# Retention attention and a snake feed-forward layer on one core: later chunks in 64x64 quads, state in SBUF, two sequences loaded whole

## The chip, the cores and the metric

The kernel runs on 1 core of one Trainium2 chip. The metric is device time in microseconds (us), lower is better. A run lists the span of the core and the mean clock granted to TensorE; runs more than 1.5% above the fastest of their kernel are called slow and are left out of comparisons. A profile covers one execution, whose span is about 1.8 us shorter than the time that the run reports.

The engines, as the profile names them: PE is TensorE (matmuls), PEld its weight loads, DVE is VectorE, ACT is ScalarE, POOL is GpSimd, SP is SyncE. In the kernel text, tiles of `psum` lie in PSUM, where the matmuls write; the others (`big`, `work`, `consts`) lie in SBUF, the working memory. The inputs are float32 and are cast to bf16 on the way in, by loads that GpSimd issues.

## The reference

Four sequences of 768 tokens, 8 heads of width 64, go through retention (linear attention with a decay for each head), and the result through a feed-forward layer with a snake activation.

```python
def _attn_ref(q, k, v):                      # each (4, 8, 768, 64)
    gamma = 1.0 - 2.0 ** (-5.0 - np.arange(H))
    for t in range(S):
        state = gamma * state + k[:, :, t] (outer) v[:, :, t]      # 64x64 for each head
        y[:, :, t] = q[:, :, t] @ state / sqrt(D)

def _moe_ref(x, w_in, w_out, alpha):         # x: 3072 tokens x 512, d_ff 2048
    h = x @ w_in
    s = np.sin(alpha * h)
    g = h + s * s / (alpha + 1e-09)
    return g @ w_out
```

(The first function is abridged: the einsums of the original are written as products.)

## The kernel before

The tokens are cut in 24 chunks of 128. The first chunk of each sequence is e0 to e3; `P` is the order of work: first the four first chunks, then chunks 1 to 5 of each sequence. A chunk's attention has four parts on TensorE: scores of the chunk with itself (`stage_A`), the part from the state of the chunks before it, the mix of masked scores with v, and the sums of k times v that go into the state (`stage_S`). All are matmuls of 64 rows or 64 columns, which run in pairs on two half tiles. The decays are divided out of v beforehand (`scale_v`) and multiplied back in when the chunk leaves PSUM (`qg`), so that the state in PSUM is a plain running sum.

```python
def load_chunk(j, names="qkv"):              # three loads of 128 partitions x 8 heads: 1024 runs each
    # ... (tiles)
    nc.gpsimd.dma_start(out=t, in_=chunk_of(src, j))

def turn(j):                                 # the transpose of q and k by DMA
    nc.sync.dma_start_transpose(out=st["qkT", j], in_=raw["qk", j].rearrange("p i h d -> p (i h d)"))

def stage_A(j):                              # scores, then the mask on DVE
    # ...
    for p in range(NP):
        for e in range(2):
            r = slice(64 * e, 64 * e + 64)
            nc.tensor.matmul(pa[:, e, p, :], qkT[r, NP + p, :], qkT[r, p, :], ...)
    nc.vector.tensor_mul(aT, pa, m)          # (rearranges cut)

def keep_S(j, ps):                           # ScalarE copies the sums from PSUM to the weights s_bd
    for e in range(2):
        r = slice(64 * e, 64 * e + 64)
        nc.scalar.copy(s_bd[(j % NCH + 1) % 2][r, :, r], ps[r, :, :])

def stage_M(j):                              # state part, mix, sums, exit to xT
    # ...
    nc.vector.tensor_mul(x, py, qg[:, c])
    if ps is not None:
        keep_S(j, ps)
```

The feed-forward (FF) work is done in groups of tiles of 128 tokens, of sizes 4, 2, 4, 4, 4, 4, 2. In each of a group's slots four FF matmuls make one hidden block (`ph`), ScalarE takes sine and square, DVE adds (`gT`), and TensorE does output matmuls (`po`) of the group before. The attention of the next group's chunks stands between slots:

```python
def phase(g, outs, att, nf=1):
    for n in range(FF // nf):
        now = Slot(g, n * nf, nf=nf).sq("A")
        for fn in att.get(n, ()):            # attention of chunks of the next group
            fn()
        now.add()
        # ... output matmuls of the group before

load_chunk(P[7])                             # GpSimd's order: loads and v decays
load_chunk(P[8])
scale_v(P[6], nc.gpsimd)
# ... loads and decays one after the other to the last chunk

phase(1, outs,                               # the two-tile group; T: transpose on TensorE, X: by DMA
      {0: [T(P[6]), X(P[8])], 1: [A(P[6])], 2: [T(P[7]), X(P[9])], 3: [A(P[7]), M(P[6])], 4: [X(P[10])],
       5: [A(P[8]), M(P[7])], 6: [X(P[11]), A(P[9]), M(P[8]), SK(e1)], 7: [M(P[9])]}, 2)
```

## Time and profile before

| | before |
|---|---|
| median of 3 runs | 219.79 us (218.58 to 219.89) |
| span of the profiled execution | 217.5 us |
| first FF matmul, last matmul (starts) | 15.49, 213.03 us |
| two-tile group starts | 48.21 us |
| the four four-tile groups after it start | 65.09, 90.94, 123.43, 155.67 us |
| last two-tile group starts | 185.54 us |

The starts are those of the first FF matmul of each group, read in the order in time of TensorE. They serve as milestones: the same matmul exists in every kernel, so the difference of two neighbouring milestones is the length of one stage, and a change of the total can be split by stage. The first stages as stretches, with the busy time of each engine:

```profile
core 0: us, PE busy (x) PEld busy (x) DVE busy (x) ACT busy (x) POOL busy (x), PEclk, DMA share, GB/s
48.20:65.10 16.90, 15.64 (x222) 12.03 (x225) 14.06 (x25) 14.40 (x33) 15.42 (x18) 1.00 2.00 161
65.10:90.90 25.80, 24.91 (x213) 12.40 (x216) 18.49 (x25) 22.63 (x41) 20.87 (x23) 1.00 1.93 149
90.90:185.50 94.60, 93.02 (x693) 45.24 (x704) 52.72 (x68) 74.38 (x129) 20.91 (x23) 1.00 0.72 81
```

From 90.9 us on, TensorE is busy nearly all the time (93.02 of 94.60).

### The profile page before, as it was taken

The page shows a single profiled execution, that of the slowest core. Times are in us where ns is not written, and L with a number is a line of the kernel's source. Part 1 is how long each engine was busy: PE and PEld are TensorE (multiplying, and loading weights), DVE is VectorE, ACT ScalarE, POOL GpSimd, SP SyncE. Part 2 cuts the span into 40 slices and gives each one's busy share as a digit, 9 for nine tenths or more (in the row PEclk, how much of TensorE's full clock was granted, in tenths as well). Part 3 has the DMA queues.
Part 4 walks back from the last instruction along what each step waited for, and adds up shares of the span by engine and source line. Part 5 has one row for each costly group of instructions (what it writes and reads, how often), then busy time and mean ns, then how long its engine had stood idle before and what let it go on. Part 6 is the DMA issues. An engine that isn't in the chain of part 4 may idle for free.

```text
span 217.5 us, 4218 instructions
## 1 busy us (share of the span) xinstructions
PE 203.8 (94%) x1634; PEld 107.5 (49%) x1661; DVE 128.1 (59%) x213; ACT 162.8 (75%) x311; POOL 90.1 (41%) x105
## 2 busy tenths in 40 slices
PE   7798899999989999999999999999999999999992
PEld 3444554467764545445455445454544544555540
DVE  4686659867895767766466566366464555233310
ACT  7678796658889999789768768777868876766610
POOL 8975335999889885896981000000000000000000
PEclk9999999999999999999999999999999999999999
DMA  9999999999999999999999146237011101111121
GB/s 132 151 193 191 205 207 164 154 207 161 164 151 182 163 120 154 112 160 175 135 188 107 23 96 77 60 60 96 7 47 51 48 0 51 48 48 48 51 94 50
DMA packets 99508, 24.67 MB, mean 113 GB/s; under 512 B 92304, under 2 KB 96416, under 8 KB 99488
## 3 DMA queue, kind: packets, MB, share of 16 engines
q0 software_dynamic: 77024, 13.37, 84.0%
q1 hardware_dynamic: 22464, 11.02, 26.4%
q8 instruction: 13, 0.21, 0.4%
q14 instruction: 7, 0.06, 0.1%
HBM read 27.27 MB, written 6.29 MB: 154 GB/s over the span
## 4 chain that ended last, share of the span: by engine, by line
PE 74%; DVE 9%; DMA 4%; POOL 4%; ACT 4%; issue 3%; POOLq 0%; ACTq 0%
PE po L304 35%; PE ph L279 31%; DMA qkr<-in_k_dram 4%; DVE gT L294 4%; PE py L247 3%; PE pa L213 2%; POOL qkr L83 2%; ACT s L282 2%; DVE aT L217 2%; PE py L251 2%; POOL vr L83 1%; DVE xT L258 1%; PE ps L227 1%; DVE s L289 1%; ACT s L287 1%
## 5 line engine op out<-in xcount | busy, mean ns | idle before, releaser
L294 DVE SCALAR_TENSOR_TENSOR gT<-s,rec_alpha,ph 128x512 bf16<-128x512 f32 (+3 forms) x120 | 74.1, 637 | 68.1 <-ACT s L287 67.5
L279 PE MATMUL ph<-xT,w_in 128*128 128x512 bf16 (+3 forms) x478 | 97.9, 336 | 1.1 <-DVE gT L294 0.6
L304 PE MATMUL po<-w_out,gT 128*128 128x512 bf16 x360 | 94.1, 379 | 3.8 <-issue 2.9
L282 ACT ACTIVATE s<-ph,alpha_sb 128x512 f32<-128x512 f32 (+3 forms) x120 | 69.6, 601 | 34.0 <-PE ph L279 33.9
L279 PEld LDWEIGHTS <-w_in 128*128 128x128 bf16 x480 | 45.5, 98 | 42.6 <-issue 2.1
L287 ACT ACTIVATE s<-s 128x512 f32<-128x512 f32 (+1 forms) x94 | 58.4, 621 | 2.6
L304 PEld LDWEIGHTS <-gT 128*128 128x128 bf16 x384 | 35.2, 98 | 38.2 <-issue 0.6
L112 POOL TENSOR_TENSOR vr<-vr,kg 128x512 bf16<-128x512 bf16 x21 | 22.0, 1056 | 12.2 <-DMA vr<-in_v_dram 12.2
L217 DVE TENSOR_TENSOR aT<-pa,mask 128x1024 bf16<-128x1024 f32 x20 | 24.4, 1220 | 0.3 <-PE pa L213 0.3
L83 POOL DMA_DIRECT2D vr<-in_v_dram x24 | 21.7, 904 | 3.0 <-DMA w_in<-in_moe_w_in_dram 1.7
L83 POOL DMA_DIRECT2D qkr<-in_q_dram x23 | 21.3, 925 | 4.0 <-DMA w_out<-in_moe_w_out_dram 1.6
L83 POOL DMA_DIRECT2D qkr<-in_k_dram x23 | 20.4, 887 | 3.8 <-DMA w_out<-in_moe_w_out_dram 3.3
L234 ACT CAST s_bd<-ps 64x256 bf16<-64x256 f32 x40 | 14.4, 360 | 2.4 <-PE ps L227 2.1
L316 ACT COPY o_sb<-po 128x512 f32<-128x512 f32 x23 | 13.1, 576 | 3.9 <-PE po L304 3.9
L258 DVE TENSOR_TENSOR xT<-py,qg 128x512 bf16<-128x512 f32 x20 | 13.7, 684 | 2.6 <-PE py L251 2.5
L328 PE MATMUL spare<-warm 128*128 128x512 bf16 x27 | 9.3, 465 | 1.4 <-DVE warm L131 1.2
L213 PEld LDWEIGHTS <-qkT 64*128 64x128 bf16 x192 | 5.4, 94 | 9.3 <-issue 7.1
L251 PE MATMUL py<-aT,vr 128*64 128x128 bf16 x192 | 9.5, 220 | 0.4 <-DVE rec_alpha L366 0.2
L213 PE MATMUL pa<-qkT 64*128 64x128 bf16 x192 | 9.5, 219 | 0.4 <-ACT qkT L186 0.2
L247 PE MATMUL py<-qkT,s_bd 128*64 128x128 bf16 x160 | 8.3, 224 | 0.7 <-DVE xT L258 0.7
L247 PEld LDWEIGHTS <-s_bd 128*64 128x64 bf16 x160 | 5.4, 109 | 4.8 <-issue 2.0
L251 PEld LDWEIGHTS <-vr 128*64 128x64 bf16 x192 | 6.9, 110 | 1.3 <-issue 1.0
(59 smaller groups left out, 68.8 us busy)
## 6 DMA issues: line engine op xcount, KB each, us to landing
out_dram<-o_sb SPq DMA_DIRECT2D x24, 256.0 KB, 2.3
vr<-in_v_dram POOLq DMA_DIRECT2D x24, 128.0 KB, 6.2
qkr<-in_q_dram POOLq DMA_DIRECT2D x23, 128.0 KB, 5.6
qkr<-in_k_dram POOLq DMA_DIRECT2D x23, 128.0 KB, 5.8
w_in<-in_moe_w_in_dram POOLq DMA_DIRECT2D x4, 512.0 KB, 11.1
w_out<-in_moe_w_out_dram POOLq DMA_DIRECT2D x4, 512.0 KB, 14.8
q<-in_q_dram SPq DMA_DIRECT2D x1, 256.0 KB, 3.4
k<-in_k_dram SPq DMA_DIRECT2D x1, 256.0 KB, 4.7
```

What stands on the lines that cost most here:

```text
L83: nc.gpsimd.dma_start(out=t, in_=chunk_of(src, j))
L112: eng.tensor_mul(raw["v", j], raw["v", j], kg[:, j % NCH, :, None].to_broadcast([128, H, D]))
L213: nc.tensor.matmul(pa[:, e, p, :], qkT[r, NP + p, :], qkT[r, p, :], start=(p == 0), stop=True, skip_group_check=True)
L217: nc.vector.tensor_mul(aT.rearrange("p e n t -> p (e n) t"), pa.rearrange("p e n t -> p (e n) t"), m)
L247: nc.tensor.matmul(py[r, p, :], s_bd[c % 2][:, p, r], qkT[:, p, :], start=(p == 0), stop=True, skip_group_check=True)
L251: nc.tensor.matmul(py[64 * e:64 * e + 64, p, :], vs[:, 2 * p + e, :], aT[:, e, p, :], start=(c == 0 and p == 0), stop=True, skip_group_che ...
L258: nc.vector.tensor_mul(x, py, qg[:, c])
L279: nc.tensor.matmul(self.ph[:, m, :], w_in[:, i, f * 128:(f + 1) * 128], xT[g][:, i, self.lo:self.hi], start=(m == 0 and i == 0), stop=(i = ...
L282: nc.scalar.activation(out=self.s[:, m, :], in_=self.ph[:, m, :], func=ACTF.Sin, scale=alpha_sb[:, f:f + 1])
L287: nc.scalar.activation(out=self.s, in_=self.s, func=ACTF.Square)
L294: nc.vector.scalar_tensor_tensor(gT[self.g][:, f, self.lo:self.hi], self.s[:, m, :], rec_alpha[:, f:f + 1], self.ph[:, m, :], op0=ALU.mult ...
L304: nc.tensor.matmul(po[g, ts], gT[g][:, f, ts * C:(ts + 1) * C], w_out[:, f, :], start=(f == 0), stop=(f == FF - 1))
```

## The change

The intent is fewer and shorter matmul bursts for attention. Queries, keys and values of the later chunks are arranged so that four 64x64 tiles of the array work at once (in the "narrow" chunks, those of sequences 0 and 1, this holds for the state part and the scores; their mix and sums stay on two half tiles); for the later chunks of sequences 2 and 3 ("wide" chunks) tokens are split in halves of 64, the empty corner of the scores is left out, and the state part is a full-array matmul. For that the rows of the result are ordered differently (so `w_in` is loaded with some halves of rows swapped), the state sits in SBUF (`s_f`, summed by DVE), and sequences 2 and 3 are loaded whole, head by head. All of one chunk's state part and mix and the next chunk's scores form one burst. Some decays go to DVE; the eighth, eleventh and twelfth chunks are transposed on TensorE (before: the seventh and eighth, the others by DMA; the fifth and sixth on TensorE in both), two early output tiles lie in the scores' PSUM banks, and the last output tile leaves in three pieces.

```diff
+    def load_seq(bt):                       # 24 loads of 64 partitions x 10 blocks: 640 runs each
+        for i, src in enumerate((q, k, v)):
+            for h in range(H):
+                # ...
+                nc.gpsimd.dma_start(out=o, in_=src[bt, h, C:, :].rearrange("(f i) d -> i f d", i=64))
@@
-        nc.gpsimd.dma_start(out=w_in[:, :, ...], in_=w_in_v[:, :, ...])
+        nc.gpsimd.dma_start(out=w_in[:, 0:2, c], in_=w_in_v[:, 0:2, c])
+        for y in range(2):
+            nc.gpsimd.dma_start(out=w_in[64 * y:64 * y + 64, 2:4, c], in_=w_in_v[64 - 64 * y:128 - 64 * y, 2:4, c])
@@ the state
+    def keep(j, py, base=256):
+        # ... first chunk: copy
+            nc.vector.tensor_add(s_f, s_f, new)
+    def hand_on(j):
+        if not wide(j + 1):
+            nc.scalar.copy(s_n[i], s_f)
+            return
+        nc.gpsimd.tensor_copy(s[half(0), :, 0:4:3], s_f[half(0)])
+        nc.gpsimd.tensor_copy(s[half(1), :, 1:3], s_f[half(1)])
@@ attention
+    def inter(j):                           # wide: 4 matmuls of the full array
+    def scores(j, tag="pa"):                # 64x64 tiles, four at a time
+    def mix(j, first=None):                 # wide: the same, narrow: half tiles; and the sums
+    def burst(old, new, first=None):
+        inter(old)
+        return {**scores(new), **mix(old, first)}
@@ GpSimd's order
+    load_chunk(P[11])
+    scale_v(P[9], nc.gpsimd)
+    load_chunk(P[12])
+    load_chunk(P[13])
+    load_seq(2)
+    load_seq(3)                             # the first wide decay and state copy come behind these
@@ the two-tile group
     phase(1, outs,
+          {0: [A(P[6]), X(P[9])], 1: [B(P[6], P[7])], 3: [B(P[7], P[8])],
+           5: [B(P[8], P[9], e1)], 6: [T(P[10])], 7: [B(P[9], P[10])]}, 2, calm=False, hold=6)
@@ the end
-    for fn in out_pieces(NG - 1, range(sizes[-1])):
+    for fn in out_pieces(NG - 1, range(sizes[-1] - 1)):
         fn()
+    last_tile(NG - 1, sizes[-1] - 1)        # 256, 128 and 128 columns
```

## The prediction

> **What bounds the kernel now.** I read the page first: the busy row, the slices and the chain of waits.
>
> ```profile
> PE 203.8 (94%) x1634; PEld 107.5 (49%) x1661; DVE 128.1 (59%) x213; ACT 162.8 (75%) x311; POOL 90.1 (41%) x105
> POOL 8975335999889885896981000000000000000000
> DMA  9999999999999999999999146237011101111121
> PE 74%; DVE 9%; DMA 4%; POOL 4%; ACT 4%; issue 3%; POOLq 0%; ACTq 0%
> L304 PE MATMUL po<-w_out,gT 128*128 128x512 bf16 x360 | 94.1, 379 | 3.8 <-issue 2.9
> ```
>
> TensorE is the bound: three quarters of the chain is its own work, at full clock. The two rows of digits say that loads and GpSimd are busy in the first 22 slices (about 120 us) and idle after. The feed-forward (FF) matmuls start every 0.216 us (four take 0.86 us in the chain), and 768 of that size are 165.8 us. They begin at 15.49 us and the last ends at about 213.3; so attention, transposes and stalls cost 198 - 166 = 32 us in that stretch. Next I read the order in time of TensorE around one attention burst in the steady part:
>
> ```profile
> 100.26 1.03 PE L279 MATMUL ph<-xT,w_in 128*128 128x512 bf16 x4
> 101.22 0.40 PE L213 MATMUL pa<-qkT 64*128 64x128 bf16 x8
> 101.55 0.41 PE L247 MATMUL py<-qkT,s_bd 128*64 128x128 bf16 x8
> 101.79 0.39 PE L251 MATMUL py<-aT,vr 128*64 128x128 bf16 x8
> 102.02 0.29 PE L227 MATMUL ps<-vr,qkr 128*64 128x64 bf16 x8
> ```
>
> The FF matmuls before it end streaming at 100.26 + 0.86 = 101.12 and FF resumes at about 102.25, so a burst takes 1.13 us. Eight matmuls of 128 columns that run in pairs on two half tiles take 0.23 us where no tile shape changes (101.79 to 102.02), which is 4 x 0.056. Where the shape changes (FF to 64x128, 64x128 to 128x64, 128x64 to FF) another 0.1 us goes, three times in the burst.
>
> The next view is VectorE (DVE), in the group of two tiles at 48 to 65 us, by stretches and in time:
>
> ```profile
> 60.00:65.00 5.00, 4.31 (x74) 3.19 (x73) 5.00 (x10) 4.17 (x11) 4.41 (x6) 1.00 1.99 151
> 61.80 1.22 DVE L217 TENSOR_TENSOR aT<-pa,mask 128x1024 bf16<-128x1024 f32 x1
> 62.94 0.68 DVE L258 TENSOR_TENSOR xT<-py,qg 128x512 bf16<-128x512 f32 x1
> 63.53 0.86 DVE L294 SCALAR_TENSOR_TENSOR gT<-s,rec_alpha,ph 128x256 bf16<-128x256 f32 x2
> 63.67 0.41 PE L247 MATMUL py<-qkT,s_bd 128*64 128x128 bf16 x8 [0.34 <-DVE xT L258]
> ```
>
> Here DVE (third busy column) is busy 5.00 of 5.00 us and TensorE waits for it. Last, GpSimd's issues, and the tail:
>
> ```profile
> 7.67 1.53 POOL L91 DMA_DIRECT2D w_in<-in_moe_w_in_dram  x2
> 41.69 0.88 POOL L83 DMA_DIRECT2D qkr<-in_k_dram  x1
> 63.14 0.94 POOL L83 DMA_DIRECT2D qkr<-in_q_dram  x1
> 213.44 0.42 DVE L313 COPY o_sb<-po 128x256 f32<-128x256 f32 x1 [6.23 <-PE po L304]
> 213.90 0.37 ACT L314 COPY o_sb<-po 128x256 f32<-128x256 f32 x1 [3.33 <-DVE o_sb L313]
> ```
>
> An issue of 1024 short runs costs GpSimd 0.88 us, one of 512 runs (w_in) 0.75. At the end two half copies stand one behind the other, then the output transfer.
>
> **What the Trainium skill says.** "TensorEngine Tiling (Array Packing)", Tiling Modes, says that 64x64 gives four independent tiles and that a change of tiling mode drains TensorE. The trace agrees on the drain (0.1 us each); it has no 64x64 tile. "TensorE: Matmul & The Clock Gate", Part 3, gives about 4 ns between the starts of matmuls on different tiles; single records of this trace show 2 to 4 ns within a pair, so four tiles should hide behind 28 ns of streaming (64 columns). The tiling page's PSUM Bottleneck section warns that tiling does nothing for PSUM evacuation; the 5.00 of 5.00 above is that case. "DMA: Bandwidth & Descriptors", SWDGE vs HWDGE vs iDMA, says GpSimd computes the descriptors in software; the 0.75 and 0.88 us fit a fixed part of about 0.61 plus 0.13 per 512 runs.
>
> **The change part by part.**
>
> 1. Attention on TensorE. For the ten later chunks of sequences 2 and 3 ("wide"), queries and keys are split in halves of 64 tokens. Per burst: state part 4 full-array matmuls, 4 x 0.056 = 0.22; scores in 64x64 quads, 2 x (0.056 + 0.028) = 0.17 because the empty upper corner is left out; mix the same 0.17; sums 4 quads x 0.028 = 0.11; two shape changes 0.2 (the state part has FF's shape). Sum 0.87, with ragged starts 0.90, against 1.13: 0.23 saved, ten times, 2.3 us. For the ten other later chunks: state part in quads 2 x 0.056 = 0.11, scores 0.22, mix 0.22, sums 0.11, three changes 0.3: 0.97, so 0.15 saved, 1.5 us. One more chunk is transposed on TensorE (8 x 0.056 = 0.45). Net -3.3 us, all on the bounding engine.
>
> 2. State. Before, PSUM held the running sum and ScalarE copied it twice per chunk (0.36 us each). Now DVE adds the chunk's sums to a copy in SBUF (128x256, about 0.43 us by the 0.68 of 128x512), and ScalarE copies once or GpSimd does it for wide chunks. ScalarE is relieved by 0.4 to 0.7 us a chunk, DVE loaded by 0.43; for wide chunks the smaller mask (768 for 1024 columns, about 0.93 for 1.22) gives 0.3 back.
>
> 3. The two-tile group. DVE there before: 16 gT of 0.475 (7.6), four masks (4.9), four exits (2.7), two copies of transposes (1.4): 16.6 us, and the group took 16.7. After: five masks (6.1), four exits (2.7), four sums (1.7), one copy (0.7), 7.6: 18.8. The last mask does not hold up the next group, so about +1 us, where TensorE's saving is lost; with the score banks of the pair of output tiles freed only after ScalarE's copies, +1.5.
>
> 4. Waits in 65 to 90 us: ScalarE was near full (9.36 of 10 in 70 to 80) and single stalls of 0.3 to 0.4 us stand before bursts. The new order (sums first, one burst per four slots, fewer ScalarE copies) should save about 1 us, less the v decay of four chunks on DVE (0.74 each, from idle time).
>
> 5. Start. FF begins at 15.5 as before. The transpose of the fourth sequence's first chunk comes one slot later and waits about 0.6 less for its load, but the next chunk's transposes wait for a load that lands at 37.5 in either kernel: no gain.
>
> 6. Tail: output in 256, 128 and 128 columns, each with its own copy and transfer; the last copy is one of 128 columns instead of two of 256 in a row. -0.8 us, less 0.1 for shorter matmuls.
>
> Sum: 219.8 - 3.3 + 1.5 - 1.0 - 0.7 = 216.3.
>
> **The rivals.** (a) GpSimd's queue becomes the bound. Ten chunks now come in 48 issues of 640 runs (64 partitions, 10 blocks) in place of 30 of 1024. By the fit one costs 0.77: 48 make 37 us against 26. Chunk loads end about 61.4 (the present times, less the four decays moved off GpSimd before then), so the last issue would end near 98.5. Behind it in GpSimd's order stand the first wide decay (1.06) and the state copies, so about 100. TensorE wants that state in the second slot of the third four-tile-era group, about 94 by my count (group two starts near 66, lasts 25.5, plus 2.6). That is a wait of 6 us and a time near 222. For it: the arithmetic. Against it: the cost for half the partitions is not in the trace and could be nearer the fixed 0.61, which ends at 92 and waits for nothing; and the change takes work off GpSimd and transposes off the DMA queue just there, as if loads had been fitted to the need. I put a third on a wait of more than 2 us. (b) DVE hides the saving: if each sum and mask in group two also lands on the path, parts 1 and 4 give only 1.5 us and the time is 218. For it: DVE would have about 24.6 us of work in a group of 25. (c) Everything overlaps: DVE's extra work falls into TensorE's output pieces, which are held back for the end of the two-tile group; then 212 to 213. (d) Quads don't run four at a time, because weight loads or banks collide: then wide bursts take about 1.5 us and the time is 221. Pairs at 28 ns with a load each in the present sums speak against it.
>
> **Range and chances.** 216.3 is the sum without (a); (c) pulls down about as often as (b) pulls up, (a) adds a tail above. I predict 216.5, range 211.5 to 223. Faster by over 2% is below 215.4: 0.40. Within 2%: 0.46. Slower, above 224.2, needs (a) in full and (b) or (d): 0.14.
>
> **What would show it.** In the changed profile: a wide burst of 0.9 us between FF matmuls, and 0.97 for others; more than 1.1 refutes part 1. DVE's busy share in 48 to 66 us at 95% or more, and that group no shorter than 17 us, carries part 3. A wait of the state part's weights on GpSimd near 94 to 100 us shows rival (a), and the length of one 64-partition issue decides it: 0.61 or 0.77. The tail from the last matmul to the end should be 3.4 us against 4.2. I am wrong if the saving comes from the start, or if a wait for loads stands in groups two or three.

## The result

The changed kernel took **233.98 us** (median of 4 runs, 233.63 to 234.09), the kernel before 219.84 us (4 runs, 218.58 to 220.38) beside it. The ratio is 1.065 (1.060 to 1.070): slower, and far outside the predicted range. A ratio here is the mean time of one kernel's fast runs over that of the other's of the same rounds, so not quite the ratio of the medians quoted.

The page of the changed kernel, as the prediction read that of before:

```profile
PE 209.7 (90%) x1965; PEld 111.3 (48%) x1965; DVE 139.2 (60%) x253; ACT 153.5 (66%) x282; POOL 103.3 (44%) x144
PE   7798899898579999960999999999999999999994
PEclk9999999999959999997699999999999999999999
PE 51%; DMA 26%; POOL 18%; issue 2%; DVE 0%; POOLq 0%; DVEq 0%
L347 PE MATMUL py<-qkT,s_w 128*128 128x128 bf16 x40 | 4.1, 228 | 7.2 <-POOL s_w L333 7.2
```

A slice is 5.8 us. The row of PE has two holes, at about 58 to 64 us (a 5) and 99 to 110 us (a 6 and a 0). The row of the granted clock, which was all nines before, has low digits at or just behind them. And TensorE's share of the chain of waits has gone from 74% to 51%; DMA and GpSimd have 44% instead of 8%. The bound has moved in the first half.

Split by milestones (us; spans of one profile each):

| stage | before | after | change |
|---|---|---|---|
| start to the two-tile group | 48.21 | 50.16 | +1.95 |
| two-tile group | 16.88 | 23.53 | +6.65 |
| first four-tile group | 25.85 | 26.08 | +0.23 |
| second | 32.49 | 40.77 | +8.28 |
| third | 32.24 | 31.46 | -0.78 |
| fourth | 29.87 | 29.18 | -0.69 |
| last two-tile group, to the start of the last matmul | 27.49 | 27.73 | +0.24 |
| start of the last matmul to the end | 4.51 | 3.39 | -1.12 |
| sum | 217.54 | 232.29 | +14.75 |

Two stages make all of it. TensorE's order in time in the first of them (after; the bracket gives the idle time ahead of the line and what ended it):

```profile
57.48 0.42 PE L363 MATMUL pa<-qkT 64*64 64x128 bf16 x16 [0.63 <-DMA qkT<-qkr]
...
60.80 0.31 PE L352 MATMUL py<-qkT,s_n 64*64 64x128 bf16 x8
65.53 0.64 PE L363 MATMUL pa<-qkT 64*64 64x128 bf16 x16 [4.42 <-DMA qkT<-qkr]
...
67.28 1.91 PE L439 MATMUL ph<-xT,w_in 128*128 128x256 bf16 x8
68.99 1.01 PE L254 MATMUL pt<-ident,qkr 128*128 128x128 bf16 x8
```

The scores of the tenth chunk (`P[9]`) wait 4.42 us for the DMA that transposes it, and those of the ninth waited 0.63 us. Where that transpose stands in SyncE's queue, after:

```profile
44.29 1.35 SPq L263 DMA_TRANSPOSE qkT<-qkr  x1
...
48.83 1.42 SPq L263 DMA_TRANSPOSE qkT<-qkr  x1
...
55.82 1.29 SPq L263 DMA_TRANSPOSE qkT<-qkr  x1
```

and before, where the line holds the ninth's and the tenth's, the latter issued at 51.59:

```profile
49.54 4.85 SPq L205 DMA_TRANSPOSE qkT<-qkr  x2
```

The landing is asked of the line of the transpose, in a window that holds the tenth chunk's alone; before, then after:

```profile
L205 SPq DMA_TRANSPOSE qkT<-qkr x1: 2803/2803/2803, 51.6 to 51.6; - x1
DMA to landing us min/median/max: 7.0/7.0/7.0
...
L263 SPq DMA_TRANSPOSE qkT<-qkr x1: 1289/1289/1289, 55.8 to 55.8; - x1
DMA to landing us min/median/max: 9.7/9.7/9.7
```

The chunk's scores come at about the same time in both kernels (60.60 before, about 60.94 wanted after). Its transpose was issued at 51.59 before and landed at 58.63, in time. After, it was issued at 55.82, as soon as the chunk's keys had landed (55.68), and landed at 65.48. The keys' load itself was issued 1.3 us later than before (47.18 for 45.84) but landed 4.2 us later (55.68 for 51.51): the transpose of the seventh chunk, the line at 44.29, which was TensorE's work before, now lies among the loads, and so does the ninth's at 48.83. Before, the first DMA transpose was issued at 49.54.

In the second stage:

```profile
101.49 1.03 PE L439 MATMUL ph<-xT,w_in 128*128 128x512 bf16 x4
109.76 0.61 PE L347 MATMUL py<-qkT,s_w 128*128 128x128 bf16 x4 [7.24 <-POOL s_w L333]
...
111.30 1.89 PE L463 MATMUL po<-w_out,gT 128*128 128x512 bf16 x4
112.98 1.63 PE L439 MATMUL ph<-xT,w_in 128*128 128x512 bf16 x4
114.45 1.03 PE L463 MATMUL po<-w_out,gT 128*128 128x512 bf16 x4
```

The first wide chunk's state part waits 7.24 us for GpSimd's copy of the state. GpSimd's own order in time shows what stands ahead of that copy:

```profile
64.84 0.88 POOL L89 DMA_DIRECT2D vr<-in_v_dram  x1 [1.87 <-DMA qkr<-in_q_dram]
65.95 0.72 POOL L104 DMA_DIRECT2D qk_seq<-in_q_dram  x1 [0.23 <-issue]
...
86.14 1.42 POOL L104 DMA_DIRECT2D v_seq<-in_v_dram  x2 [1.44 <-DMA qk_seq<-in_k_dram]
...
100.00 2.14 POOL L104 DMA_DIRECT2D qk_seq<-in_k_dram  x3 [2.34 <-DMA qk_seq<-in_q_dram]
102.11 5.73 POOL L104 DMA_DIRECT2D v_seq<-in_v_dram  x8
107.75 1.16 POOL L142 TENSOR_TENSOR v_seq<-v_seq,kgq 128x512 bf16<-128x512 bf16 x1
108.74 0.51 POOL L332 CAST s_w<-s_f 64x256 bf16<-64x256 f32 x1
```

The 48 head-by-head loads are issued from 65.95 to 107.84 us, 0.72 us each (5.73 for eight), and besides that GpSimd itself waits for loads to land before it can issue more (2.34, 1.44 us; in this trace no load is issued while eight others are still in flight). Only then come the decay and the copies.

The clock: in both stages the matmuls behind the hole run at half speed for a few us. Four matmuls of 512 columns take 0.86 us elsewhere; from 111.30 to 112.98 they take 1.68, from 112.98 to 114.45 1.47, and from 114.45 0.86 again. Eight of 256 columns took 1.71 (67.28 to 68.99) for 0.88, and the eight transposes after them 0.85 for 0.45. Asked in stretches of 1 us, the granted clock is 0.50 from 63.0 to about 69.8 us and from about 107.4 to 114.2 us. The Trainium skill, "TensorE: Matmul & The Clock Gate", Part 1, says that after an idle window of about 3.4 us the array falls back to half clock until it has been busy for such a window. The trace agrees on the whole: gaps of 4.4 and 7.2 us do it, gaps up to 1.6 us in the fast runs below do not. But in the first place the half clock begins only 1.9 us after the last matmul has ended (61.11 us), so that a whole idle window did not come before it. The mean clock agrees: it is 0.971 or 0.978 in the runs of the changed kernel and at least 0.995 in the fast runs of the kernel before, and half of one 3.4 us window in 232 us is 0.007 (an estimate from the page's figure), so that 0.971 stands for four windows, two for each place. By the lengthened lines, summed from the end of the gap to the first line at full speed, the half clock costs 1.9 us in the first place and 2.1 in the second.

So the waits with their after-effects make 5.05 + 1.9 us in the first stage, which became 6.65 longer, and 7.24 + 2.1 in the second, which became 8.28 longer. By this sum the stages would otherwise have been 0.3 and 1.1 us shorter than before; what they are when the waits are really gone, the experiments show.

What the quads did, from the chain of waits, where a wide burst in the steady part lies between FF and output matmuls:

```profile
118.93 0.86 PE ph L439 x4
119.79 0.22 PE py L347 x4
120.02 0.18 PE pa L372 x4
120.49 0.13 PE py L314 x16
120.61 0.97 PE po L463 x4
```

From 119.79 to 120.61 is 0.82 us; the burst took 1.13 before. The first part follows FF without a gap, as FF has its shape. And the tail: the copies and the transfers of the last tile.

```profile
227.38 0.37 ACT L485 COPY o_sb<-poh 128x256 f32<-128x256 f32 x1 [1.16 <-PE poh L481]
229.22 0.29 DVE L487 COPY o_sb<-poh 128x128 f32<-128x128 f32 x1 [0.60 <-PE poh L481]
```

Only one copy, of 128 columns and 0.29 us, stands behind the last matmul, where two half copies in a row (0.42 and 0.37) stood before: 1.1 us less in the table, of which 0.16 is that the last matmul itself is shorter (0.22 us for 0.38).

DVE in the two-tile group, which the prediction made the bound:

```profile
50.20:73.70 23.50, 18.12 (x266) 12.83 (x265) 15.66 (x28) 14.10 (x30) 18.88 (x24) 0.85 2.31 163
73.70:99.80 26.10, 25.63 (x266) 12.71 (x265) 22.58 (x35) 21.00 (x37) 19.98 (x28) 1.00 1.96 146
```

It is busy 15.66 us of 23.5: not the bound, since the group waits for the DMA. In the next group DVE has 22.58 us of 26.1 (18.49 before) and TensorE is busy 25.63 of 26.10.

### The profile page after: what moved, and what is told of

It is laid out like the page before. It is cut to its first block, busy times and chain, and to the rows that moved or that the text cites. A ratio compares the mean times of both kernels' runs of the same rounds, so it can differ in the third digit from the quotient of the medians.

```text
span 232.3 us, 4897 instructions
## 1 busy us (share of the span) xinstructions
PE 209.7 (90%) x1965; PEld 111.3 (48%) x1965; DVE 139.2 (60%) x253; ACT 153.5 (66%) x282; POOL 103.3 (44%) x144
## 4 chain that ended last, share of the span: by engine, by line
PE 51%; DMA 26%; POOL 18%; issue 2%; DVE 0%; POOLq 0%; DVEq 0%
PE po L463 26%; PE ph L439 20%; DMA w_out<-in_moe_w_out_dram 9%; POOL qk_seq L104 7%; DMA qkr<-in_q_dram 5%; DMA qk_seq<-in_q_dram 4%; DMA qk_seq<-in_k_dram 3%; POOL qkr L89 3%; POOL v_seq L104 3%; DMA vr<-in_v_dram 3%; DMA w_in<-in_moe_w_in_dram 3%; POOL vr L89 3%; PE poh L481 2%; POOL vr L142 1%; PE py L347 1%
## 5 line engine op out<-in xcount | busy, mean ns | idle before, releaser
L381 DVE TENSOR_TENSOR aT<-pa,maskq 128x768 bf16<-128x768 f32 x10 | 9.6, 957 | 8.6 <-PE pa L376 7.5
L89 POOL DMA_DIRECT2D vr<-in_v_dram x14 | 12.7, 907 | 4.5 <-DMA qkr<-in_q_dram 1.9
L104 POOL DMA_DIRECT2D qk_seq<-in_k_dram x16 | 11.5, 742 | 3.7 <-DMA qk_seq<-in_q_dram 3.1
L367 DVE TENSOR_TENSOR aT<-pa,mask 128x1024 bf16<-128x1024 f32 x10 | 12.2, 1217 | 1.6 <-PE pa L363 1.6
L89 POOL DMA_DIRECT2D qkr<-in_k_dram x13 | 11.7, 900 | 2.4 <-DMA w_out<-in_moe_w_out_dram 1.7
L89 POOL DMA_DIRECT2D qkr<-in_q_dram x13 | 11.9, 918 | 1.7 <-DMA w_out<-in_moe_w_out_dram 1.2
L104 POOL DMA_DIRECT2D v_seq<-in_v_dram x16 | 11.5, 758 | 2.6 <-DMA qk_seq<-in_k_dram 2.5
L104 POOL DMA_DIRECT2D qk_seq<-in_q_dram x16 | 11.5, 745 | 1.5 <-issue 1.2
L142 POOL TENSOR_TENSOR v_seq<-v_seq,kgq 128x512 bf16<-128x512 bf16 x10 | 10.5, 1054 | 0.7
L347 PE MATMUL py<-qkT,s_w 128*128 128x128 bf16 x40 | 4.1, 228 | 7.2 <-POOL s_w L333 7.2
```

The lines of the kernel that those rows point to most:

```text
L104: nc.gpsimd.dma_start(out=o, in_=src[bt, h, C:, :].rearrange("(f i) d -> i f d", i=64))
L142: eng.tensor_mul(t, t, by[:, j % NCH, :, None].to_broadcast([128, H, D]))
L367: return {"mask": lambda: nc.vector.tensor_mul(aT.rearrange("p e n t -> p (e n) t"), pa.rearrange("p e n t -> p (e n) t"), mask_bc)}
L381: return {"mask": lambda: nc.vector.tensor_mul(aT, pa[:, :, 0:384].rearrange("p e (m t) -> p e m t", m=2), maskq[:, None, None, :].to_broa ...
```

## The experiments

The expectations speak of **G**, that the order of GpSimd's queue makes the wait for the state: take the first state copy and its decay off that queue and the wait is gone. The rival **D** says that the DMA engines are the bound, so that the wait would stay under another name. A further question is what the two waits are worth singly and together, as a wait that is removed can come back in the next one. And then, what is left when all are gone: does the change gain anything? All runs were timed beside the kernel before on the same chip. Where no other is named, the edit is to the changed kernel.

### The first wide state off GpSimd

```diff
-        nc.gpsimd.tensor_copy(s[half(0), :, 0:4:3], s_f[half(0)])
-        nc.gpsimd.tensor_copy(s[half(1), :, 1:3], s_f[half(1)])
+        copy = nc.scalar.copy if j == 2 * NCH else nc.gpsimd.tensor_copy
+        copy(s[half(0), :, 0:4:3], s_f[half(0)])
+        copy(s[half(1), :, 1:3], s_f[half(1)])
-        return lambda: scale_v(j, nc.gpsimd if wide(j) or j % NCH == 0 else nc.vector)
+        return lambda: scale_v(j, nc.gpsimd if j != 2 * NCH + 1 and (wide(j) or j % NCH == 0) else nc.vector)
```

> The changed kernel, with the v decay of the first wide chunk on VectorE and the two copies of its state on ScalarE, so that neither stands behind GpSimd's 48 load issues. Theory G (GpSimd's issue order holds TensorE at the first wide state): the 7.2 us wait and about 1.4 us of half clock after it go, less what the next chunk's decay, still behind the issues, takes back: 224 to 228 us. Rival D (the loads and transposes themselves land late, GpSimd's order only coincides): TensorE stops at the same burst, at the next chunk's transposed queries, and the time stays within 2 us of 234.

Measured: 225.52 us (224.02 to 227.1), ratio 1.028 (1.022 to 1.034). The wait for the state is gone from the list of TensorE's waits, whose first line is now

```profile
PE pa L364 <- DMA qkT<-qkr: 4.3, 1, 4.3
```

(total, times, longest). The second four-tile group took 31.72 us, below the 32.49 of before and 9.05 less than in the changed kernel. That is the 7.24 of the wait and 1.8 more, near the 2.1 put down to the half clock. Theory G holds and D falls for this wait: the data were there.

### The tenth chunk transposed on TensorE

```diff
-          {0: [A(P[6]), X(P[9])], 1: [B(P[6], P[7])], 3: [B(P[7], P[8])],
+          {0: [A(P[6])], 1: [B(P[6], P[7])], 3: [B(P[7], P[8])], 4: [lambda: stage_T(P[9], nc.scalar)],
```

> The changed kernel, with the tenth chunk in order (the last of the two-tile group's bursts) transposed on TensorE and not by DMA. It takes away the 4.4 us wait near 61 us, and one transpose from among the loads. Theory G: GpSimd's queue is the longer chain, so the gain is only what its issues come earlier, 2 to 3 us (231 to 232), and the wait for the first wide state grows to about 10 us. Rival: the two waits add up, and the gain is the whole 4.4 us plus the half clock after it, about 6 us (228).

Measured: 233.05 us (231.88 to 233.64), ratio 1.061 (1.057 to 1.065), some 0.4% better than the changed kernel, which is not clear of noise (1.060 to 1.070 there). The two-tile group went from 23.5 to 19.75 us, and still the end moved by less than 1 us: TensorE came earlier to the state and waited longer for it.

```profile
108.83 0.61 PE L347 MATMUL py<-qkT,s_w 128*128 128x128 bf16 x4 [8.68 <-POOL s_w L333]
```

The state was ready at about 108.8 for 109.7: GpSimd's queue goes at its own pace, whatever TensorE does. To take away a wait ahead of another one that ends when it will is worth next to nothing.

### Both

> Both edits of the two runs before. Theory G: more than the sum of the two single gains, because each wait hides the other: 218 to 222 us. Rival (two independent waits): the gains of the two single runs simply add.

Measured: the two fast runs of four took 221.19 and 222.57 us, ratio 1.012 (1.007 to 1.016); two others, 228.07 and 227.83, are slow, with a clock of 0.984 and 0.992, were not traced and are left out. Such clocks stood beside long waits above, so one of the waits may have come back in them; that is not shown. In per cent of the time before: 3.7 for the first edit, 0.4 for the second, 5.3 for both, so the waits cost some 12 us together (5.3% of 219.5). The second edit is worth 0.4% while the state is late and 1.7% when it is not: the wait for the state hid the one for the transpose. As 5.3 rests on two runs of four, it is good that the next run, which has both edits and more, gives 4.9 with four fast runs of four. The profile (a fast run) has no wait over 1.2 us in the middle of the kernel. What is there now, in the two-tile group, are waits for DVE to free PSUM:

```profile
59.97 1.03 PE L440 MATMUL ph<-xT,w_in 128*128 128x256 bf16 x8 [1.09 <-DVE gT L455]
...
64.96 1.03 PE L440 MATMUL ph<-xT,w_in 128*128 128x256 bf16 x8 [1.17 <-DVE gT L455]
...
66.85 1.90 PE L464 MATMUL po<-w_out,gT 128*128 128x512 bf16 x8
```

Each follows a group of transposes on TensorE (at 58.05 and 62.96), whose tile in PSUM comes from the same four buffers as FF's. The first comes with the repair; the second is of the kind that the prediction's third part feared, and the wait for the DMA had covered it. The group takes 19.15 us against 16.88. (The last line is where FF's output goes on after a narrow burst.)

### All of sequence 2 off GpSimd

The edit of "both", with the condition widened to all five wide chunks of sequence 2: decays on DVE, state copies on ScalarE.

```diff
+        copy = nc.scalar.copy if j < 3 * NCH else nc.gpsimd.tensor_copy
+        return lambda: scale_v(j, nc.gpsimd if j >= 3 * NCH else nc.vector)
```

> The tenth chunk transposed on TensorE, and all five wide chunks of sequence 2 with decay on VectorE and state copies on ScalarE. Theory G: nothing of sequence 2 waits for GpSimd; 213 to 217 us, faster than the kernel before, as the wide bursts take 0.82 us for 1.13. Rival D: TensorE then waits for the transposed queries of the second and third wide chunks, and the time is no better than that of the run with both edits.

Measured: 222.56 us (222.42 to 223.59), ratio 1.016 (1.013 to 1.019). A miss: no better than "both". Nothing more was waiting on GpSimd once the first state was off it: no wait for it is left in the trace of "both". Rival D has the time right; of the waits that it named, 0.7 us for a wide chunk's transposed queries is all that the trace shows.

### The seventh chunk on TensorE instead of the tenth

If the seventh chunk's DMA transpose is what makes the loads of the tenth land late, taking that one out of the way should bring the tenth's in time. The edit is against the run before it.

```diff
-    turn(P[6])
     # ...
-    fill(9)
+    fill(5)
+    stage_T(P[6], nc.scalar)
+    fill(4)
-          {0: [A(P[6])], 1: [B(P[6], P[7])], 3: [B(P[7], P[8])], 4: [lambda: stage_T(P[9], nc.scalar)],
+          {0: [A(P[6]), X(P[9])], 1: [B(P[6], P[7])], 3: [B(P[7], P[8])],
```

> As the run with all of sequence 2 off GpSimd, but the chunk taken from the DMA transposes is the seventh in order (as in the kernel before) and not the tenth. If a DMA transpose among the loads is what delays everything behind it, the tenth chunk's own DMA transpose now lands in time, the two-tile group loses the two 1.2 us stops at PSUM tiles that the transpose on TensorE brought in, and it is 219 to 221 us. If the number of bytes alone sets the landing, the 4 us wait near 61 us is back: 226 us.

Measured: 220.75 us (220.29 to 221.08), ratio 1.006 (1.002 to 1.010), the best of the repaired kernels, and still not below the kernel before. The tenth chunk's transpose was now issued at 51.76 and landed at 59.36, in time, though nothing was done to it. The reason lies in its load of keys. With one transpose less among the loads it landed at 51.50; in "both" it was issued at the same time and landed at 54.24. The wait that the rival, the bytes alone, called for is not there. The load in this run, then in "both":

```profile
L89 POOL DMA_DIRECT2D qkr<-in_k_dram x1: 883/883/883, 46.0 to 46.0; - x1
DMA to landing us min/median/max: 5.5/5.5/5.5
...
L89 POOL DMA_DIRECT2D qkr<-in_k_dram x1: 883/883/883, 45.7 to 45.7; - x1
DMA to landing us min/median/max: 8.5/8.5/8.5
```

The two-tile group took 17.73 us. Its largest remaining waits:

```profile
63.68 1.03 PE L440 MATMUL ph<-xT,w_in 128*128 128x256 bf16 x8 [1.46 <-DVE gT L455]
...
91.02 0.25 PE L373 MATMUL pa<-qkT 64*64 64x128 bf16 x4 [1.55 <-DMA qkT<-qk_seq]
```

The second is the transpose of the first wide chunk. A wide chunk needs loads of all its heads, and a whole-sequence load brings all chunks of the sequence at once, so the first chunk is there only when the last head has landed.

Stage by stage, where these kernels stand (us):

| stage | before | after | first state | tenth chunk | both | seventh chunk |
|---|---|---|---|---|---|---|
| to the two-tile group | 48.21 | 50.16 | 50.38 | 50.32 | 49.44 | 49.58 |
| two-tile group | 16.88 | 23.53 | 23.43 | 19.75 | 19.15 | 17.73 |
| first four-tile group | 25.85 | 26.08 | 26.00 | 27.33 | 27.10 | 27.78 |
| second | 32.49 | 40.77 | 31.72 | 42.54 | 31.96 | 32.20 |
| third and fourth | 62.11 | 60.64 | 60.64 | 60.64 | 60.63 | 60.82 |
| rest | 32.00 | 31.12 | 31.03 | 31.12 | 31.12 | 31.19 |

Read the last column against the first: 1.4 + 0.85 + 1.9 us lost up to the end of the first four-tile group, 0.3 + 1.3 won in the next three, 0.8 in the rest. Sum: +1.8, as the spans (219.3 against 217.5) say.

### w_in in 4 loads instead of 12

The run "all of sequence 2", with `w_in` loaded as before. The rows are then in the wrong order, so the result is wrong (relative error 1.30); the work is the same.

```diff
-        nc.gpsimd.dma_start(out=w_in[:, 0:2, c], in_=w_in_v[:, 0:2, c])
-        for y in range(2):
-            nc.gpsimd.dma_start(out=w_in[64 * y:64 * y + 64, 2:4, c], in_=w_in_v[64 - 64 * y:128 - 64 * y, 2:4, c])
+        nc.gpsimd.dma_start(out=w_in[:, :, c], in_=w_in_v[:, :, c])
```

> As the run with all of sequence 2 off GpSimd and the tenth chunk on TensorE, with w_in loaded in four pieces as before and not in twelve. The result is wrong on purpose (rows of w_in are not swapped). If the twelve pieces delay the loads behind them (at most eight are in flight), the chunk loads land 1 us or more earlier and the time falls by about 1 us; if the order of bytes alone counts, nothing changes.

Measured: 222.16 us (221.88 to 222.49), ratio 1.013 (1.009 to 1.016), against 222.56 with the split, on another chip. At most 0.4 us: the eight more issues at the start are not what makes the two-tile group start late (at 49.50 us here, at 49.44 in "both", with the split).

### No wide chunks

The wide form taken out: sequences 2 and 3 loaded in chunks as before (30 loads of 1024 runs for 48 of 640) and computed as the others; decays on DVE, states on ScalarE follow from that.

```diff
     def wide(j):
-        return j % NCH > 0 and j // NCH >= 2
+        return False
-    load_seq(2)
-    load_seq(3)
+    for n in range(14, NJ):
+        load_chunk(P[n])
```

> The changed kernel without the wide form: all twenty later chunks by the narrow quad path, loaded chunk by chunk (30 issues for 48), decay on VectorE, state copies on ScalarE. Theory G: the wait for GpSimd is gone, the one for the tenth chunk's transpose stays, and ten bursts take about 1.02 us for 0.82: 225 to 228 us, near the run that only took the first wide state off GpSimd. If the wide form pays in itself, this is 2 us slower than that run; if the 48 issues cost the loads more than the form saves, it is faster.

Measured: the fast runs took 225.93 and 229.29 us, ratio 1.038 (1.029 to 1.046); two more were slow, and the profile is of one of those, so only the kind of its waits is used. The wait for the state is gone here too, without any copy having been moved by hand. What is left:

```profile
PE pa L363 <- DMA qkT<-qkr: 9.4, 3, 5.0
```

Three waits for DMA transposes. With the wide chunks away, GpSimd is free and the change is still well slower than before: the order of the transposes is a fault of its own. Whether the wide form pays in itself stays open: the mean of the two fast runs is 2 us above the run without the first state on GpSimd, as the expectation said, but these two lie 3.4 us apart.

### Wide chunks for sequence 3 only, with and without earlier transposes

Sequence 2 loaded in chunks, sequence 3 whole, the seventh chunk on TensorE; and the DMA transposes in the four-tile groups placed one chunk earlier.

```diff
-        return j % NCH > 0 and j // NCH >= 2
+        return j % NCH > 0 and j // NCH >= 3
-    load_seq(2)
+    for n in range(14, 19):
+        load_chunk(P[n])
-            if n + 2 < NJ:
-                at(a - 1, X(P[n + 2]))
+            if n == 10:
+                at(0, X(P[12]))
+            if n + 3 < NJ:
+                at(a - 1, X(P[n + 3]))
```

> Wide form for sequence 3 alone; sequence 2 narrow and loaded chunk by chunk; seventh chunk on TensorE; from the four-tile groups on, each DMA transpose is issued one chunk (four slots) earlier. If the waits come from asking for sequence 2 as a whole, and for transposes five slots ahead of their use, then neither the state wait nor the waits for transposes are there, the group that starts near 67 us takes 26 us and not 27.8, and the time is 217.5 to 219.5, level with or a little under the kernel before. If the DMA queue is short whatever the order, it stays at 220.5 or above.

> The same without the earlier issue of the transposes (five slots ahead, as in the changed kernel). If the lead is what counts, waits for transposes of 1 to 3 us stand in the two groups from 67 to 128 us and the time is 1 to 3 us above the run with the earlier issue; if only the whole-sequence load counts, the two runs agree within 0.5 us.

The second leaves out the last hunk. Measured: 221.01 us (219.77 to 223.22, the highest a slow run), ratio 1.007 (1.002 to 1.011), with the earlier transposes; 222.96 us (221.56 to 223.38), ratio 1.014 (1.009 to 1.018), without. The lead of one chunk is worth about 1.5 to 2 us (the two intervals overlap by a little). It was expected to be level with the kernel before and missed: the first four-tile group took 27.28 us against 25.85, with one wait of 1.3 us for a transpose left there and one of 0.7 in the two-tile group.

### The tail alone

The kernel before, with only the last output tile in pieces of 256, 128 and 128 columns.

```diff
-    for fn in out_pieces(NG - 1, range(sizes[-1])):
+    for fn in out_pieces(NG - 1, range(sizes[-1] - 1)):
         fn()
+    last_tile(NG - 1, sizes[-1] - 1)
```

> The kernel before, with the last output tile in 256, 128 and 128 columns. From the two traces the stretch from the last group's start to the end is 0.9 us shorter in the changed kernel; here the same: ratio 0.996, with nothing else moved. If the shorter stretch came from elsewhere in the last group, under 0.3 us.

Measured: 218.62 us (6 runs, 217.39 to 218.81) against 219.47 on the same chip, ratio 0.995 (0.992 to 0.998). By the rule of 2% that is the same, but the interval leaves out 1. The end of its profile has the same copies as that of the changed kernel:

```profile
212.01 0.37 ACT L331 COPY o_sb<-poh 128x256 f32<-128x256 f32 x1 [1.16 <-PE poh L327]
213.85 0.29 DVE L333 COPY o_sb<-poh 128x128 f32<-128x128 f32 x1 [0.60 <-PE poh L327]
```

This is the only version that beat the kernel before, and the changed one with it.

## Why the prediction was wrong

The prediction said 216.3 for the sum and gave a range to 223; the kernel took 234. What failed is the path: the prediction's sum has TensorE's own work and DVE's on it, and the changed kernel waits for two queues of DMA issues. GpSimd's queue, which holds the state back (rival (a), left out of the sum), made a wait of 7.24 us, and SyncE's queue of transposes, which no step has, waits of 5.05 us. The steps, one by one:

1. **Attention on TensorE (-3.3).** The mechanism was right and so were the sizes of the bursts: 0.82 us measured for the predicted 0.90 (wide), and 1.02 (65.83, where FF's streaming ends, to 66.85 in "both") for the predicted 0.97 (narrow). The rival (d), that quads do not run four at a time, is refuted. But the sum was too large, because the early groups could not use it: 0.8 and 0.7 us were won in the third and fourth four-tile groups and 1.1 in the second by the sum above (0.8 in the run without its wait), about 2.5 us in all, and none before.

2. **State.** Its work did move as described. Its place in the queue was the fault, under (a) below.

3. **The two-tile group (+1.5).** The sign was right, the size and the reason only in part. The count of 18.8 us was too high, as the same count for the kernel before (16.6) already was: the stretches show 14.06 before (the group took 16.88, not 16.7) and 15.20 of 17.73 in "seventh chunk", where nothing else holds the group up for long. That is 86%, below the 95% that the prediction named as its sign, so DVE is not the bound of the group; TensorE waits for it at single places, 1.1 to 1.5 us each, behind transposes. The group costs 0.85 us more in "seventh chunk". In the changed kernel itself the group was 6.65 us longer for another reason.

4. **Waits in 65 to 90 us (-1.0).** Wrong: that group took 26.08 us for 25.85. TensorE's idle time fell there from 0.9 to 0.5 us, but it had 0.7 us more work, the eight transposes of part 1 among it.

5. **Start.** Right for the first FF matmul (15.50 for 15.49), wrong for the stretch after it, which is 1.95 us longer. The trace shows 0.51 us of it as the scores' wait for ScalarE to empty the output tiles in the scores' banks, and 0.29 for DVE's exit at its end. The rest was not isolated.

6. **Tail (-0.7).** Right: from the end of the last matmul it is about 3.2 us for 4.1 (forecast: 3.4 for 4.2), and 0.85 us between the medians when done alone.

**Rival (a), which the prediction gave a third**, is where it failed most. The prediction wrote "That is a wait of 6 us and a time near 222" and left it out of the sum, since "the cost for half the partitions is not in the trace". The mechanism came true, and its two inputs were too kind. An issue took 0.72 us, near the 0.77 of the fit and not the 0.61 that was hoped for. But the head-by-head loads began at 65.95 instead of 61.4 and ended at 107.84 instead of 98.5, as GpSimd also waits for its own loads to land, a wait that no term had: about 7 of these 42 us are gaps between issues (48 times 0.72 is 35). TensorE came later too, which kept the wait at 7.24 us. The half clock behind a long gap, about 2 us, was a missing term as well. Taking this one thing out gave 8.5 us back between medians (233.98 to 225.52).

**The wait for DMA transposes was missing altogether**, 5.05 us with 1.9 of half clock behind it. Part 5 counted a transpose with its load at the start, but no step asked when the tenth chunk's transpose could be issued and how long it takes among loads, though SyncE's view of the kernel before has the answer in the same window (51.59 to 58.63, 7.0 us). Its last sentence said it would be wrong "if a wait for loads stands in groups two or three"; that is near to what happened.

What is shown: both waits, by the runs that take each and both away. The seventh-chunk run shows that a transpose earlier in the queue made the tenth's late, by way of its loads. What is only read from traces: the cost of the half clock, and how the transposes and loads share the DMA engines. What stays open: most of the 1.4 us that the best repaired kernel loses ahead of the two-tile group, and whether quads with another order of loads could win; no run here combined them so that they did.

## What to carry to other kernels

When a change puts work behind a queue of issues, count that queue's own time to the end, with the waits of the issuing engine for loads in flight, and compare it with the time at which the bounding engine will ask; do this for every new producer, the DMA transposes too. A wait can hide another one that comes before it, when it ends at its own time whatever TensorE does: here 3.7% and 0.4% singly were 5.3% together, so test them together before calling one of them harmless. A saving on the bounding engine is only worth what the stages can use that are still bound by it, here about 2.5 us of 3.3, while the two new waits in front of it cost 16 by the lines of the trace, and 12 when both were taken away, as smaller waits then came to light.

## What the Trainium skill lacked or had wrong

- "DMA: Bandwidth & Descriptors", Anatomy of one DMA, calls descriptor generation "small, variable". For loads of many short runs it is the cost that counts: GpSimd was held 0.72 us by an issue of 640 runs and 0.88 us by one of 1024, and 48 of the former took it 42 us with its waits. The page gives no cost by the number of runs. Nor has it a limit of loads in flight: no load of the changed kernel's trace was issued while eight were in flight, and 57 of 104 were issued as the eighth (whether the chip or the program sets this is not shown).
- The same page, Queues, rings and completion order, says that each DMA engine takes turns between the queues that have work. It gives no latency for a DMA transpose among loads of another queue. Here one took 9.7 us from issue to landing at 55.82 among loads, and 3.1 us at 118.67 when the loads were over (landed 121.76).
- "TensorEngine Tiling (Array Packing)", Tiling Modes, says that a change of tiling mode drains the array, without a figure: about 0.1 us in the kernel before. A full-array state part behind FF, where the mode stays, paid none (FF's streaming ends at 119.79 and the state part starts there).
- "TensorE: Matmul & The Clock Gate", Part 1, puts the fall to half clock after at least one idle window of about 3.4 us. Here it came 5 us after the last matmul in one place but 1.9 us after it in the other (61.11 to 63.0), with TensorE busy for 1.53 us of the 3.4 us before it.
